# Weight loads of the expert stage in halves, with at most three halves on the way

## The chip, the core and the metric

The kernel runs on one core of a Trainium2 chip. The metric is the device time of one execution in microseconds (us). The core's engines work side by side, each through its own instruction stream: PE (TensorE, matrix products; PEld is its loading of weights), DVE (VectorE), ACT (ScalarE), POOL (GpSimd) and SP (SyncE). SP does nothing here but start transfers. All transfers between the chip's memory (HBM) and the core's memory (SBUF), whoever starts them, run on the same 16 DMA engines.

## The reference

Causal attention is followed by a mixture of experts with a capacity. Cut to what matters:

```python
# q, k, v: (8, 12, 448, 64); w1: (8, 768, 1024); w2: (8, 1024, 768); capacity 80
attn = softmax(causal(q @ k.T / 8)) @ v          # per batch and head
x = attn.transpose(0, 2, 1, 3).reshape(3584, 768)
logits = x @ w_gate                               # 8 experts
expert_idx = argmax(logits); gate_w = softmax(logits)[expert_idx]
for e in range(8):
    tok = the (at most) 80 tokens of expert e with the largest gate_w
    h = maximum(x[tok] @ w1[e], 0.0)
    out[tok] = gate_w[tok, None] * (h @ w2[e])    # all other rows stay zero
```

## The kernel before, in words

The first three quarters are the attention: scores, exponentials, transposes and products for 48 pairs of heads, in an order written out by hand, with the rows of x written to `xs` in HBM (L617), zeros to `out` (L305) and the gating worked out between. From about 355 us on come the eight experts, and only this stage is touched.

**Weights.** Each expert has a `w1` (768 x 1024) and a `w2` (1024 x 768) in f32. Both are cut into two *pieces* of 3072 columns on 128 partitions, 1.5 MB each (`PW`, `PIECES`: three chunks of 128 rows of `w1`, or four of `w2`): 32 pieces in all. `piece()` takes the next of ten buffers named `wraw` in turn. The first five pieces come in small parts during the attention (`piece_parts`, L213); five more come whole between 322 and 338 us; the other 22 are loaded by `split_pieces` while experts run. A load starts on SP's queue (`load_piece`, L202) when the piece that held its buffer ten pieces earlier has been used up.

**Splitting.** TensorE multiplies in f16 here, so each chunk of a piece becomes a high part `wh` (ScalarE, L1156) and a low part `wl` (VectorE, L1141, the scaled weight minus the high part). There are 12 buffers for high parts and 11 for low parts, so the two engines run ahead of PE by that many chunks. A few chunks (`whole`) are not split but multiplied in f32 straight from `wraw` (L1206).

**An expert.** GpSimd gathers the expert's 80 rows of x (`gather`, L1173) into `xg`. PE transposes them (`xtp`, L1187), ScalarE and VectorE split them into `xh` and `xl` (L1191, L1192). `layer1` makes the products with `w1`, three for each block of 128 x 128 (high by high, high by low, low by high: L1213, L1215, L1216). `hidden` applies the maximum and splits again (`hh` L1232, `hl` L1233). `layer2` does the same with `w2` into `op`. `outputs` scales (`yt`, L1279), transposes back (`ytp`, L1287), multiplies by the gate's weight (`yo`, L1291), and GpSimd scatters the 80 rows into `out` (L1294). Layer 1 of one expert runs before layer 2 of the expert before it.

**What sets the order.** PE's order in this stage is written out (`manual_schedule`). For the other engines a planner orders the instructions at build time, with its own costs, among those whose inputs and buffers it expects to be ready. Each engine then runs its list in order and waits on semaphores; a transfer raises its semaphore when all of it has landed. SP's list in this stage holds the 22 loads and the wait for the kernel's end.

Of the kernel before, what the change touches and what calls it, by code (L numbers as in the profile page):

```python
# [52 lines left out]
def attention_then_moe(  # L53
# [12 lines left out]
    nc = tc.nc  # L66
# [65 lines left out]
    for r in range(2):  # L132
        t = akeep.tile([P, OFF_L + NT * P], F32, name=f"prob{r}")
# [7 lines left out]
    for r in range(2):  # L141
        t = akeep.tile([P, NT, PH * P], F32, name=f"vt{r}")
# [20 lines left out]
        [(c, NT - 1, None) for c in (2, 1, 3, 0)],  # L163
    ]
    TB = 4

    PW = 3072
# [16 lines left out]
    def piece():  # L186

        e, which, c, k = PIECES[len(wload)]
        x = len(wload) % (WBUF + WMORE)
        pool, bufs = (wpool, WBUF) if x < WBUF else (wmore[0], WEARLY) if x < WBUF + WEARLY else (wmore[1], WMORE - WEARLY)  # L190
        t = pool.tile([P, k, PW // k], F32, name="wraw", tag="w", bufs=bufs)
        wload.append(t)
        return t, (w1 if which == 1 else w2)[e, :, c:c + k, :]

    def load_piece(behind=None):

        if len(wload) < len(PIECES):
            t, src = piece()
            if behind is not None:
                with tc.issue_after(behind.ins):  # L200
                    nc.gpsimd.memset(t[:, 0, 0:1], 0.0)
            nc.sync.dma_start(t, src)  # L202

    def piece_parts():

# [752 lines left out]
    with tc.manual_schedule():  # L958
# [26 lines left out]
        for i, pr in enumerate(pairs):  # L985
# [21 lines left out]
            for k in range(SLOTS):  # L1007
                behind = []
                if k < SLOTS - 1:
                    work, after = scores[k]  # L1010
                    turn, copy, x = turns[TSLOT.index(k)] if turns and k in TSLOT else (None, None, "a")
# [5 lines left out]
                    behind = [f for f in ((copy, after) if x == "a" else (after, copy)) if f]  # L1017
# [11 lines left out]
                if i == n - 2 and len(wload) >= WBUF and not parts and k in (0, 2, 4):  # L1029
                    load_piece()  # L1030
# [10 lines left out]
        while len(wload) < WBUF:  # L1041
            load_piece()
        while len(wload) < WBUF + WEARLY:
            load_piece()
# [40 lines left out]
        for i, x in enumerate(ROW_ENGINES):  # L1085
            g, t = divmod(i, NT)
# [30 lines left out]
    def whole(e, which, c):  # L1117

        if e >= E - 2:
            return False  # L1120
        return c == NC2 - 1 if which == 2 else c >= (NC1 // 2 if e == 0 else NC1 - 1)
# [11 lines left out]
    def split_pieces(m):  # L1133

        first = done[0]
        done[0] += m
        order, lows = [], []

        def low(l, src, h):
            with tc.issue_after((low_after or last_of)[-1].ins):  # L1140
                return nc.vector.scalar_tensor_tensor(out=l, in0=src, scalar=SW, in1=h, op0=ALU.mult, op1=ALU.subtract)  # L1141

        for i in range(first, first + m):
            while len(wload) <= i:
                load_piece()
            e, which, c, k = PIECES[i]
            for j in range(k):
                src = wload[i][:, j, :]
                order.append(c + j)
                if whole(e, which, c + j):  # L1150
                    parts_of[(e, which, c + j)] = (src,)
                    continue
                h = wsplit.tile([P, PW // k], F16, name="wh", tag="wh", bufs=HIS, padded_shape=[P, max(F, D)])
                l = wsplit.tile([P, PW // k], F16, name="wl", tag="wl", bufs=LOS, padded_shape=[P, max(F, D)])
                with tc.issue_after(batches[-1].raised.ins):
                    nc.scalar.activation(h, src, AF.Copy, scale=SW)  # L1156
                lows.append((l, lambda l=l, src=src, h=h: low(l, src, h)))
                parts_of[(e, which, c + j)] = (h, l)
        return order, lows

    def split_now(m):
        order, lows = split_pieces(m)
        for _, f in lows:
            f()
        return order
# [135 lines left out]
    for s in range(NSL):  # L1301
# [15 lines left out]
        with tc.manual_schedule(engines={mybir.EngineType.PE}):  # L1317
            for e in range(E + 1):
                if e < E:
                    u = units[e]  # L1320
                    if e == 0:

                        order, lows = split_pieces(n1)
                        u.order = order[NC1 // 2:] + order[:NC1 // 2]
                        units[1].order, more = split_pieces(n1)

                        with tc.issue_after(g.ins):
                            nc.gpsimd.memset(lows[0][0][:, 0:1], 0.0)
                        for nx in units[1:AHEAD]:
                            gather(nx)  # L1330
                        for _, f in lows:
                            low_after.append(f())
                        inputs(u)
                        low_after.append(u.xl)
                        for _, f in more:
                            f()
                    elif e > 1:
                        u.order = split_now(n1)
# [62 lines left out]
```

## Time and profile before

| | |
|---|---|
| time, median of 3 runs (lowest to highest) | 480.67 us (479.31 to 481.21) |
| the profiled execution: its time, its span | 479.74 us, 477.7 us |
| granted TensorE clock | 0.997 |
| busy, share of the span: PE, DVE, ACT, POOL | 93%, 86%, 83%, 67% |
| weight pieces loaded whole | 27, of 1536 KB, median 15.5 us from issue to landing |
| of these, while experts run | 22, issued from 360.2 to 432.7 us |
| moved in all | 120.88 MB, mean 253 GB/s |

The span runs from the first to the last instruction of the profiled execution; the device time is about 2 us longer. The shares are means over the attention and the experts, which have different limits, so a change in one stage is to be read from that stage's stretch of the span. A PE that counts as busy need not be at its peak, because its matrix products overlap and their ends are modelled.

### The profile page before, as it was taken

The page shows a single profiled execution, that of the slowest core. Times are in us where ns is not written, and L with a number is a line of the kernel's source. Part 1 is how long each engine was busy: PE and PEld are TensorE (multiplying, and loading weights), DVE is VectorE, ACT ScalarE, POOL GpSimd, SP SyncE. Part 2 cuts the span into 40 slices and gives each one's busy share as a digit, 9 for nine tenths or more (in the row PEclk, how much of TensorE's full clock was granted, in tenths as well). Part 3 has the DMA queues.
Part 4 walks back from the last instruction along what each step waited for, and adds up shares of the span by engine and source line. Part 5 has one row for each costly group of instructions (what it writes and reads, how often), then busy time and mean ns, then how long its engine had stood idle before and what let it go on. Part 6 is the DMA issues. An engine that isn't in the chain of part 4 may idle for free.

```text
span 477.7 us, 14801 instructions
## 1 busy us (share of the span) xinstructions
PE 444.4 (93%) x5290; PEld 341.8 (72%) x5290; DVE 412.1 (86%) x1264; ACT 398.4 (83%) x1075; POOL 319.9 (67%) x384
## 2 busy tenths in 40 slices
PE   3999989999999999999999999999989999998894
PEld 1676666767766776776677677777549998988894
DVE  6888798978987997897799789889479999999982
ACT  5998889879888887988888798888587999988982
POOL 7999999887987988798798879860254265401101
PEclk9999999999999999999999999999999999999998
DMA  7758998889669579866956886549938999999921
GB/s 219 178 148 230 278 313 235 248 248 297 184 195 293 159 224 264 245 187 196 291 159 218 257 253 181 186 134 337 424 125 272 392 390 387 390 424 428 418 73 43
DMA packets 43001, 120.88 MB, mean 253 GB/s; under 512 B 6146, under 2 KB 23810, under 8 KB 39472
## 3 DMA queue, kind: packets, MB, share of 16 engines
q1 hardware_dynamic: 41712, 116.21, 75.0%
q0 software_dynamic: 1056, 3.51, 2.4%
q8 instruction: 41, 0.67, 0.6%
q14 instruction: 32, 0.26, 0.2%
q10 hardware_dynamic: 160, 0.23, 0.2%
HBM read 96.36 MB, written 23.99 MB: 252 GB/s over the span
## 4 chain that ended last, share of the span: by engine, by line
PE 73%; DVE 10%; POOL 6%; issue 4%; ACT 4%; DMA 2%; POOLq 0%; SPq 0%; DVEq 0%; ACTq 0%
PE tp L466 14%; PE xp L496 13%; PE sp L424 6%; PE sp L425 5%; PE hp L1206 3%; ACT prob L449 3%; DVE ns L446 3%; PE rt L594 3%; PE hp L1215 3%; PE hp L1216 3%; PE hp L1213 3%; PE op L1213 3%; PE op L1215 3%; DMA qk<-k_t 2%; PE op L1216 2%
## 5 line engine op out<-in xcount | busy, mean ns | idle before, releaser
L449 ACT ACTIVATE prob<-ns,nb 128x128 f32<-128x128 f32 (+3 forms) x336 | 177.3, 530 | 35.6 <-DVE nb L446 34.0
L446 DVE CUSTOM_DVE_ANT_0 ns<-sp,mask 128x384 f32<-128x384 f32 (+2 forms) x288 | 116.0, 414 | 27.5 <-PE sp L425 15.8
L466 PE MATMUL tp<-ident,prob 128*128 128x128 f32 x768 | 119.9, 277 | 2.8 <-ACT prob L449 2.4
L478 ACT COPY PT<-tp 128x512 f32<-128x512 f32 x182 | 104.1, 572 | 12.3 <-PE sp L424 6.2
L396 POOL TENSOR_TENSOR qk<-qk,qk 128x448 f16<-128x448 f32 x92 | 97.4, 1078 | 13.3 <-DVE qk L388 7.1
L1141 DVE SCALAR_TENSOR_TENSOR wl<-wraw,wh 128x768 f16<-128x768 f32 (+1 forms) x98 | 97.9, 1059 | 5.2 <-ACT wh L1156 2.4
L466 PEld LDWEIGHTS tp<-ident,prob 128*128 128x128 f32 x768 | 89.6, 142 | 16.4 <-ACT prob L449 4.9
L496 PE MATMUL xp<-PT,vt 128*64 128x448 f32 (+3 forms) x768 | 91.1, 380 | 0.0
L1156 ACT ACTIVATE wh<-wraw 128x768 f16<-128x768 f32 (+1 forms) x98 | 84.7, 922 | 5.0 <-PE hp L1216 2.1
L496 PEld LDWEIGHTS xp<-PT,vt 128*64 128x64 f32 x768 | 53.8, 137 | 42.7 <-issue 22.6
L424 PE MATMUL sp<-qk 128*128 128x384 f16 (+2 forms) x288 | 75.7, 279 | 8.3 <-ACT qk L356 6.1
L425 PE MATMUL sp<-qk 128*128 128x384 f16 (+2 forms) x288 | 78.3, 278 | 1.6 <-DVE qk L350 1.6
L1215 PEld LDWEIGHTS <-wh 128*128 128x128 f16 x668 | 66.7, 100 | 4.4 <-issue 4.3
L1213 PEld LDWEIGHTS <-wh 128*128 128x128 f16 x668 | 67.1, 101 | 2.3 <-issue 2.3
L1294 POOL DMA_INDIRECT out<-yo,idx x8 | 21.4, 2676 | 68.2 <-ACT yo L1291 65.1
L1216 PEld LDWEIGHTS <-wl 128*128 128x128 f16 x668 | 66.7, 100 | 0.5 <-issue 0.5
L449 ACT ACTIVATION_READ_ACCUMULATOR prob<-ns,nb 128x1 f32 x336 | 64.3, 191 | 0.0
L391 POOL TENSOR_TENSOR qk<-qk,qk 64x448 f16<-64x448 f32 x46 | 51.3, 1115 | 4.1 <-POOL qk L350 0.6
L392 POOL TENSOR_TENSOR qk<-qk,qk 64x448 f16<-64x448 f32 x46 | 49.6, 1079 | 3.3
L385 POOL CAST qk<-qk 64x896 f16<-64x896 f32 x40 | 43.0, 1074 | 4.8 <-PE sp L437 3.6
L424 PEld LDWEIGHTS <-qk 128*128 128x128 f16 x288 | 28.5, 99 | 16.8 <-issue 7.3
L1213 PE MATMUL op<-hh,wh 128*128 128x80 f16 x324 | 37.1, 202 | 2.1 <-issue 2.1
(190 smaller groups left out, 899.8 us busy)
## 6 DMA issues: line engine op xcount, KB each, us to landing
wraw<-w SPq DMA_DIRECT2D x27, 1536.0 KB, 15.5
qk<-k_t SPq DMA_DIRECT2D x92, 224.0 KB, 5.5
out<-mask_l SPq DMA_DIRECT2D x56, 192.0 KB, 4.5
qk<-q_t SPq DMA_DIRECT2D x23, 448.0 KB, 4.3
vt<-v_t SPq DMA_DIRECT2D x24, 384.0 KB, 5.9
xs<-xr SPq DMA_DIRECT2D x42, 192.0 KB, 1.9
wraw<-w SPq DMA_DIRECT2D x24, 256.0 KB, 5.9
vt<-v_t SPq DMA_DIRECT2D x24, 64.0 KB, 5.6
```

The costliest lines, as they stand in the source:

```text
L396: nc.gpsimd.tensor_tensor(out=k_lo[j][:, i], in0=kf[j][:, i], in1=k_hi[j][:, i], op=ALU.subtract)
L424: nc.tensor.matmul(sp[:, 0:w], qx[:, p, t * P:w], kx[:, p, 0:w], start=True, stop=False)
L425: nc.tensor.matmul(sp[:, 0:w], qx[:, p, t * P:w], lx[:, p, 0:w], start=False, stop=True)
L446: pr.masked = nc.vector.tensor_tensor_reduce(out=ns[:, 0:w], in0=sp[:, 0:w], in1=m, scale=-1.0 / 8.0, scalar=HUGE, op0=ALU.add, op1=ALU.mi ...
L449: nc.scalar.activation(pr.P[:, off:off + w], ns[:, 0:w], AF.Exp, bias=nb, scale=-1.0, accum_out=total)
L466: nc.tensor.transpose(pr.tp[:, i], pr.P[:, off:off + P], ident)
L478: copy(dst, src)
L496: state["pe"] = nc.tensor.matmul(xp[rows, 0:w], st["vt"][:, c, p * P + j * DH:p * P + (j + 1) * DH], pr.PT[:, j, n0:n0 + w], start=(c == 0 ...
L1141: return nc.vector.scalar_tensor_tensor(out=l, in0=src, scalar=SW, in1=h, op0=ALU.mult, op1=ALU.subtract)
L1213: nc.tensor.matmul(o, wh[:, ws], ah[:, c, :], start=(x == 0 and i % per == 0), stop=False, skip_group_check=True)
L1215: nc.tensor.matmul(o, wh[:, ws], al[:, c, :], start=False, stop=False, skip_group_check=True)
L1216: nc.tensor.matmul(o, wl[:, ws], ah[:, c, :], start=False, stop=(x == n - 1), skip_group_check=True)
```

## The change

A piece that is loaded by `split_pieces` (22 of 32) goes in two transfers of 1536 columns, 0.75 MB each, instead of one; in HBM and in SBUF the 12 KB of a partition become two runs of 6 KB. Each of these halves waits on SP until the third half ahead of it in the list has landed, so that at most three halves are on the way at once. The first three don't wait. The wait for the buffer stays. Pieces loaded earlier are untouched.

```diff
+    HALVES = 3
...
-    def load_piece(behind=None):
+    on_way = []
+
+    def load_piece(behind=None, few=False):
 
         if len(wload) < len(PIECES):
             t, src = piece()
             if behind is not None:
                 with tc.issue_after(behind.ins):
                     nc.gpsimd.memset(t[:, 0, 0:1], 0.0)
-            nc.sync.dma_start(t, src)
+            if not few:
+                nc.sync.dma_start(t, src)
+                return
+            to, of = (x.rearrange("p k f -> p (k f)") for x in (t, src))
+            for x in (slice(0, PW // 2), slice(PW // 2, PW)):
+                got = nc.sync.dma_start(to[:, x], of[:, x])
+                if len(on_way) >= HALVES:
+                    tc.add_manual_dep(got.ins, on_way[-HALVES].ins.name, mybir.DependencyInfo(
+                        mybir.DependencyClass.Sync, mybir.DependencyReason.DATA), reason="halves on the way")
+                on_way.append(got)
...
             while len(wload) <= i:
-                load_piece()
+                load_piece(few=True)
```

## The prediction

> **What bounds the kernel now.** I read the page first (how busy the transfer engines are by slice), then the chain that ended last, then the stretches between its "issue" entries, then who waited for whom in the expert stage, then the weight loads.
>
> ```profile
> span 477.7 us, 14801 instructions
> DMA  7758998889669579866956886549938999999921
> ```
>
> The change touches only the expert stage, from 360 us on (slices 31 to 40). There the transfer engines are busy nine tenths and more until slice 38. In the chain, cut to 380:478 us (start, length, what), PE is the carrier, and entries named "issue" come back in it:
>
> ```profile
> 404.84 0.64 issue
> ...
> 411.38 0.39 issue
> ...
> 418.21 0.85 issue
> ...
> 436.55 1.47 issue
> ...
> 449.19 1.28 issue
> ...
> 456.42 0.25 issue
> ```
>
> "issue" means that PE waited for no semaphore that the profile shows. The ends of these entries (405.48, 411.77, 419.06, 438.02, 450.47) are a clue. Here are the stretches between such ends, with the instructions that PE and its weight loader ran in each:
>
> ```profile
> 398.74:405.48 6.74, 6.10 (x128) 5.96 (x129) 6.74 (x7) 6.26 (x10) 5.10 (x1) 1.00 1.01 361
> 405.48:411.77 6.29, 5.90 (x127) 5.80 (x128) 6.29 (x10) 5.43 (x10) 3.31 (x2) 1.00 1.01 420
> 411.77:419.06 7.29, 6.44 (x128) 6.33 (x128) 7.29 (x9) 6.54 (x10) 3.25 (x1) 1.00 1.02 376
> ...
> 438.02:444.21 6.19, 6.13 (x128) 6.02 (x128) 5.40 (x7) 5.04 (x7) 0.00 (x0) 1.00 1.03 431
> ...
> 457.00:461.00 4.00, 4.00 (x113) 3.99 (x112) 2.42 (x4) 3.68 (x8) 0.92 (x1) 1.00 0.23 66
> ```
>
> Columns: stretch, length, busy time and count of PE, PEld, DVE, ACT, POOL, granted clock, share of the transfer engines, GB/s. Each stall comes after 128 + 128 = 256 instructions, at full clock. The transfer queues show what else happens once per 256 instructions: of the stretch 425.31:438.02 (two periods), and of the tenth of a microsecond 435.5:435.6, the rows of queue 8 are
>
> ```profile
> q8 instruction: 2, 0.03, 1.1%
> ...
> q8 instruction: 1, 0.02, 67.6%
> ```
>
> One block of 0.02 MB of instructions starts at 435.5 and PE goes on at 438.02, some 2.5 us later. So while weights stream, PE is paced by the fetching of its own code: 6.2 to 7.3 us per 256 instructions. Once the weights are in (457:461) it runs 225 instructions in 4.00 us, 256 in 4.55, with no stall of that kind.
>
> Why is the fetch slow? The scatters, which share the transfer engines too, show it: first one beside the weight stream, then one without it (instruction, landing); then the transfers that ran between issue and first scatter packet, beside the stream (429.99:434.3) and without (469.2:470.6).
>
> ```profile
> L1294 POOL DMA_INDIRECT out<-yo,idx x1: 1226/1226/1226, 430.0 to 430.0; - x1
> ...
> DMA to landing us min/median/max: 8.5/8.5/8.5
> ...
> DMA to landing us min/median/max: 3.0/3.0/3.0
> ...
> DMA packets 168, 1.86 MB, mean 431 GB/s; under 512 B 17, under 2 KB 17, under 8 KB 17
> ...
> q1 hardware_dynamic: 168, 1.86, 102.3%
> ...
> DMA packets 0, 0.00 MB, mean 0 GB/s; under 512 B 0, under 2 KB 0, under 8 KB 0
> ```
>
> Beside the stream the scatter's descriptors are written by 431.2, and no scatter packet (q0) starts before 434.3: over 3 us. Without it, they are written by 470.1 (0.9 us) and the first comes after 470.6, in the next window: about 0.5. The stream adds some 2.6 us. One of its packets takes 16 x 4.31 x 1.023 / (168 - 17) = 0.47 us for 12 KB, so a newcomer waits behind 5 or 6 of them.
>
> Who loses by PE's pace? Waits in 360:468 us (waiter, what it waited for, total, times, longest) and the sum row of 360:468.2:
>
> ```profile
> DVE wl L1141 <- ACT wh L1156: 2.4, 3, 1.9
> ACT yo L1291 <- PE ytp L1287: 2.4, 3, 1.3
> ...
> ACT wh L1156 <- PE hp L1216: 2.1, 5, 0.8
> ...
> ACT yt L1279 <- PE op L1206: 2.0, 3, 1.1
> ...
> ACT wh L1156 <- PE op L1216: 1.9, 5, 0.7
> ...
> DVE wl L1141 <- ACT yt L1279: 0.6, 1, 0.6
> ...
> sum 108.20, PE 101.45 PEld 99.65 DVE 104.38 ACT 95.11 POOL 29.82; mean PE 101.45 PEld 99.65 DVE 104.38 ACT 95.11 POOL 29.82
> ```
>
> VectorE is the next bound, and close: 104.38 of 108.20 us busy, 3.82 idle. Of that, 3.0 (2.4 + 0.6) is behind ScalarE, whose own waits are for PE to free a buffer or deliver a product. No engine waits for a weight load.
>
> **The change part by part.** *22 loads become 44 halves.*
>
> ```profile
> L202 SPq DMA_DIRECT2D wraw<-w x22: 327/328/1005, 360.2 to 432.7; - x22
> ...
> DMA to landing us min/median/max: 8.0/17.0/25.1
> ...
> q1 hardware_dynamic: 3168, 34.60, 88.4%
> ```
>
> (The last row is of 360.15:457.72, when they run.) 22 more issues of 0.33 us are 7 us on SP, which issues nothing else here and has 97: nothing. *Packets shrink from 12 KB to 6 KB.* Their rate has two bounds: none lost; or the fixed part from the small packets of 200:300 us:
>
> ```profile
> q1 hardware_dynamic: 10938, 21.16, 72.1%
> ```
>
> Those are 16 x 100 x 0.721 / 10938 = 0.105 us each, completion marks included, for 1.9 KB. A line through both gives 0.035 us per KB and 0.04 fixed, so 8 more packets per engine and load cost 22 x 8 x 0.04 = 7 us at most. Packets there met others on the same engines, so I take the low side, 2 us more streaming.
>
> *Each half waits for the landing of the third ahead.* Queued behind that wait on SP are weight halves alone, and who waits for them are wh, wl and the unsplit products. At a landing two halves are still queued, 2 x 8 x 0.235 = 3.7 us of work. The turnaround to be hidden has two bounds:
>
> ```profile
> DMA to landing us min/median/max: 2.5/7.0/25.1
> ...
> DMA to landing us min/median/max: 23.6/23.6/23.6
> ...
> q1 hardware_dynamic: 2538, 27.85, 89.6%
> ```
>
> The first row is of all weight transfers; its shortest, 192 KB, took 2.5 us, of which 0.45 is moving: 2.0 fixed. The last counts 360.15:438.53, up to the landing of the 17th load (26.74 MB): 27.85 - 26.74 = 1.1 MB had been moved beyond it, 2.6 us at 420 GB/s, and with about 1 us from issue to first packet 3.6. Both are under 3.7, the upper just so. I take no bubble, because the average need is only 34.60 MB in 97.6 us, 355 GB/s, where three halves per (3.6 + 1.9) us give 430.
>
> *Cover for later landings.* The load issued at 410.6 landed 23.6 later (second row above), at 434.3, and its first rows were read at 436.8; the last, issued at 432.7, landed 25.0 later at 457.7 and was read from 463.1:
>
> ```profile
> 436.07 1.57 ACT L1156 ACTIVATE wh<-wraw 128x768 f16<-128x768 f32 x2
> ...
> 460.15 5.96 ACT L1156 ACTIVATE wh<-wraw 128x768 f16<-128x768 f32 x8
> ```
>
> (Second of the two and fifth of the eight.) So 2.5 us of cover at the tightest and 5.4 at the end, and a half more, 1.9 us, since the first rows need the first half alone. The 2 us are hidden; if 7 came instead, the rest would be paid.
>
> *What a newcomer waits behind.* If it waits behind a number of packets, 5 or 6 of 0.235 us cost 1.3 us instead of 2.6, and the fetch period drops from 6.2 to about 4.9. If it waits behind a number of bytes, nothing changes. I take the first: the two added delays are both near six packets, and in one row set bytes would do as well, so this is the step with the least behind it. How much is needed? PE ran 2219 + 2219 instructions in 360:468.2, 17.3 blocks; to keep out of VectorE's way (104.4 us) it needs 6.0 us per block on average, and now takes 6.2 to 7.3 while streaming. So 0.5 us would do in most blocks.
>
> Here a rule of the Trainium skill speaks against me. "Runtime: NRT & Kernel Launch", Instruction fetch mechanics, says that code is refilled in 16 KiB blocks of 256 instructions and that crossing a block is mostly hidden. The block size agrees with the 128 + 128 above; "hidden" does not, by the 0.25 to 1.47 us entries. If it held, the forecast would be the no-change rival.
>
> **Sum.** With PE out of the way VectorE gets back what it spends behind ScalarE: 3.0 of its 3.82 us. PE's whole "issue" time is not the gain, for VectorE then ends last; after its last wl nothing changes. The profiled execution took 479.74 us (span 477.7): 476.7. The median of the runs is 0.93 above it (480.67), so 477.7.
>
> **The rivals.** *No change (480.7).* The fetch waits behind bytes, or behind whole loads that are always present; PE stalls as before, and the loads stay hidden by the 2.5 us. For it: the engines stay as full as before. Against it: nothing in the trace, only the missing test with small packets. A part of the gain (478.5 to 480) counts here too.
>
> *Slower (486).* The window of three is too short: the turnaround is not 3.6 but 5.5 us, because each completion queues the way the scatter's first packet does (2.6 more, less what overlaps). Then three halves (2.36 MB) per 5.5 + 1.9 = 7.4 us give 319 GB/s, 34.60 MB take 108 us instead of 97.6, and of the 11 us the cover of 5.4 hides half: 480.7 + 5.5, about 486. It decides from a round of 6.6 us on, where 2.36 MB gives the 355 GB/s needed. For it: completion is already 2.6 us late. Against it: in the stretches where the stream is slowed by gathers, so are the two halves that cover.
>
> The Trainium skill, "DMA: Bandwidth & Descriptors", Bandwidth, asks for transfers of 1 MiB and more (its 1 MB row is 341 GB/s); by that alone 34.60 MB would take an estimated 101 us, inside the cover. No run here shows a half yet.
>
> *The change doesn't act.* If SP's own buffer waits already kept fewer than three halves on the way, the window would do nothing; but landings 17 us after issue at 4.4 us per load say four loads were queued. The halving acts in any case.
>
> **How the numbers follow.** Forecast 0.50 (with 475.5 to 478.3 as its own range: all 3.8 idle us gained and a median as low as the profiled run, or half of them); no change or a part 0.34; slower 0.16. Half a percent, 2.4 us, is about what runs of this kernel can tell from no change. The range runs from 475.5 to 485: it leaves out the worse half of the slow case and a sliver below.
>
> **What would show it.** Right: "issue" entries between 380 and 456 us shrink to few or none, stretches of 256 instructions take under 6 us, scatters beside the stream land in 6 to 7 us, ScalarE's waits for PE and VectorE's idle time (3.82) mostly vanish, the last wl ends about 3 us earlier. Wrong: stalls after every 256 instructions as before (no change); waits of wh or wl for a weight load, and a transfer share under 0.95 between 370 and 440 (slower).

## The result, and the profile after

The changed kernel takes 484.59 us (median of 4 runs, 484.23 to 485.77), the kernel before on the same chip 480.01 us (4 runs, 479.31 to 481.21). The ratio is 1.0082, with a 95% interval of 1.0057 to 1.0106: slower by 0.8%, where 477.7 us was forecast. The profiled execution took 484.23 us. In this kernel's lines, everything behind the diff stands 12 lines further down than before: `wh` is L1168, `wl` L1153, `xh` L1203, `xl` L1204; the halves are issued at L210.

From the page of the changed kernel:

```profile
span 482.2 us, 14857 instructions
...
DMA  7757997799769569777956967549839999999961
...
wraw<-w SPq DMA_DIRECT2D x44, 768.0 KB, 6.9
```

The transfer engines are now busy into slice 39, one slice longer. A half takes 6.9 us from issue to landing (median). The rows of line 210, and of the weight queue from the first issue to the last landing, 360.63:468.0:

```profile
L210 SPq DMA_DIRECT2D wraw<-w x44: 327/328/424, 360.6 to 461.2; - x44
...
DMA to landing us min/median/max: 5.3/6.9/9.6
...
q1 hardware_dynamic: 6336, 34.61, 87.9%
```

The same 34.6 MB need 107.4 us instead of 97.6, 322 GB/s instead of 355, and the last landing is 10.3 us later. What SP waited for, and who waited in the expert stage (345:482; the last two rows are PE's in 430:470):

```profile
SPq L210 <- DMA wraw<-w: 79.4, 40, 3.6
...
SPq L210 <- DVE wl L1153: 12.3, 5, 8.1
```

```profile
DVE wl L1153 <- ACT wh L1168: 5.4, 6, 1.4
ACT wh L1168 <- DMA wraw<-w: 4.8, 8, 1.5
...
PE hp L1225 <- ACT xh L1203: 4.0, 2, 3.1
PE hp L1227 <- DVE xl L1204: 1.5, 2, 1.0
```

All but the first three and one of the 44 halves waited at the window, and `wh` now waits for weight loads, which it did not do before. The stretches 380:430 and 430:460, first of before, then of the changed kernel, show when it went wrong:

```profile
380.00:430.00 50.00, 47.19 (x1005) 46.19 (x1001) 49.55 (x57) 45.11 (x70) 20.18 (x7) 1.00 1.01 399
430.00:460.00 30.00, 26.91 (x615) 26.30 (x614) 26.69 (x31) 26.05 (x39) 3.35 (x3) 1.00 0.87 362
```

```profile
380.00:430.00 50.00, 47.46 (x1009) 47.02 (x1008) 50.00 (x59) 44.78 (x71) 23.12 (x6) 1.00 0.99 363
430.00:460.00 30.00, 23.88 (x507) 23.24 (x506) 25.19 (x29) 24.68 (x36) 1.95 (x2) 0.91 0.98 361
```

Until 430 us the forecast's signs appear, but they are worth little: VectorE has no idle time at all (50.00 of 50.00), and before it idled only 0.45 us there, most of its 3.82 us coming after 430. Meanwhile only 363 GB/s arrive instead of 399, and the cover is eaten up. After 430 PE runs 507 products where it ran 615, and the granted clock is 0.91. In the chain the place looks like this (start, length, what), followed by ScalarE's list (ACT), in the view in order of time:

```profile
422.88 6.57 DMA wraw<-w
429.47 6.91 DMA wraw<-w
436.44 6.11 DMA wraw<-w
442.56 7.51 DMA wraw<-w
...
450.18 1.07 ACT wh L1168
...
455.21 0.66 DVE xl L1204
...
455.91 0.23 PE hp L1227
```

```profile
450.18 2.00 ACT L1168 ACTIVATE wh<-wraw 128x1024 f16<-128x1024 f32 x2 [1.47 <-DMA wraw<-w]
...
452.61 1.58 ACT L1168 ACTIVATE wh<-wraw 128x768 f16<-128x768 f32 x2
454.09 0.55 ACT L1203 ACTIVATE xh<-xtp 128x480 f16<-128x480 f32 x1
```

Four halves follow one another in the chain, each issued as the third ahead of it landed: the loads are the path from 422.9 to 450.1. ScalarE stands idle for 1.47 us at a late half; its waits of this kind add up to 4.5 us in 430:470. Behind it in its list, after four chunks of `wh` and one of `hh`, is `xh` of the next expert, small and independent of that load; PE can start nothing before `xh` and `xl`. So PE does almost nothing from 451.00 to 455.91, and then runs on half a clock (PE's busy time and count come first, the granted clock third from the end):

```profile
451.00:455.91 4.91, 0.84 (x7) 0.59 (x7) 4.64 (x7) 4.81 (x8) 0.00 (x0) 0.84 0.96 340
455.91:460.81 4.90, 4.90 (x72) 4.87 (x72) 4.90 (x6) 3.81 (x6) 0.00 (x0) 0.50 0.95 325
460.81:465.00 4.19, 4.19 (x104) 4.15 (x103) 2.92 (x5) 3.61 (x7) 0.91 (x1) 0.96 1.02 394
```

4.07 us of PE are lost in the first row and 2.45 (half of 4.90) in the second, 6.5 us together. The span grew by 4.5; against the loss stand the shorter stalls of PE, but the balance is not worked out further here.

The Trainium skill, "TensorE: Matmul & The Clock Gate", Part 1, says that the clock is halved after an idle window of about 3.4 us, until PE has been busy for about as long. The rows agree: 4.9 us with little work, then 4.9 us at 0.50, then 0.96. Worked out from the three rows, (1 - 0.84) x 4.91 / 0.5 + 4.90 + (1 - 0.96) x 4.19 / 0.5, the half clock lasted some 6.8 us, and in the first 1.6 of them PE still waited. A wait that idles PE for so long is paid for a second time.

### The profile page after: what moved, and what is told of

Its sections match the earlier page's. It is cut to its first block, busy times and chain, and to the rows that moved or that the text cites. A ratio compares the mean times of both kernels' runs of the same rounds, so it can differ in the third digit from the quotient of the medians.

```text
span 482.2 us, 14857 instructions
## 1 busy us (share of the span) xinstructions
PE 446.0 (92%) x5290; PEld 343.9 (71%) x5290; DVE 412.9 (86%) x1264; ACT 397.3 (82%) x1075; POOL 321.6 (67%) x384
## 4 chain that ended last, share of the span: by engine, by line
PE 61%; DVE 12%; DMA 12%; ACT 6%; issue 4%; POOL 3%; SPq 1%; POOLq 0%; DVEq 0%; ACTq 0%
PE tp L478 13%; PE xp L508 12%; DMA wraw<-w 8%; PE sp L436 5%; PE sp L437 4%; DMA qk<-k_t 4%; ACT prob L461 4%; DVE ns L458 3%; PE hp L1218 3%; PE rt L606 3%; PE hp L1227 2%; PE sp L446 2%; PE gp L558 2%; PE hp L1228 2%; PE hp L1225 2%
## 5 line engine op out<-in xcount | busy, mean ns | idle before, releaser
L1153 DVE SCALAR_TENSOR_TENSOR wl<-wraw,wh 128x768 f16<-128x768 f32 (+1 forms) x98 | 97.7, 1060 | 7.0 <-ACT wh L1168 5.4
L1168 ACT ACTIVATE wh<-wraw 128x768 f16<-128x768 f32 (+1 forms) x98 | 85.4, 925 | 7.6 <-DMA wraw<-w 4.8
L1227 PEld LDWEIGHTS <-wh 128*128 128x128 f16 x668 | 67.7, 101 | 5.1 <-issue 5.0
L1228 PEld LDWEIGHTS <-wl 128*128 128x128 f16 x668 | 67.7, 101 | 4.6 <-issue 4.6
L1306 POOL DMA_INDIRECT out<-yo,idx x8 | 23.0, 2881 | 70.2 <-ACT yo L1303 67.1
L1225 PEld LDWEIGHTS <-wh 128*128 128x128 f16 x668 | 68.2, 102 | 0.0
L1225 PE MATMUL hp<-xh,wh 128*128 128x80 f16 x320 | 38.3, 207 | 4.0 <-ACT xh L1203 4.0
L1227 PE MATMUL hp<-xl,wh 128*128 128x80 f16 x320 | 37.7, 207 | 4.0 <-DVE xl L1204 4.0
```

What stands on the lines that cost most here:

```text
L1225: nc.tensor.matmul(o, wh[:, ws], ah[:, c, :], start=(x == 0 and i % per == 0), stop=False, skip_group_check=True)
L1227: nc.tensor.matmul(o, wh[:, ws], al[:, c, :], start=False, stop=False, skip_group_check=True)
```

## The experiments

The changed kernel does three things: it halves the loads, limits them to three on the way, and, since the planner sees other transfers, reorders some rows of VectorE and ScalarE near the end (expert 6's `hh` and `hl` move behind expert 7's second `w1` piece). Theories: the window is too short (the slower rival); the order is to blame; small packets are. Beside them stands the open step of the prediction: does a newcomer wait behind packets or behind bytes? The kernel before took 480.5 us beside the first four, 481.06 beside the next four and 480.41 beside the last two.

**Halves without a window.**

```diff
-    HALVES = 3
+    HALVES = 99
```

> The halves alone: 44 loads of 0.75 MB, none waits for a landing (only for its buffer). Every engine's order is that of the changed kernel. If the window of three is what cost the 4.6 us (theory W: a round of three halves takes 6.1 to 7.5 us where 6.6 would just do), the loads move 34.6 MB in under 98 us again, no engine waits for a weight load, and the time is 477 to 481: 478 if smaller packets also shorten the fetch of PE's instructions, 480 if they don't. If the halves themselves are slow, by their packets (theory P) or by the order that the planner makes of them (theory O), it stays at 483 to 485.

479.65 us, ratio 0.9987 (0.9972 to 1.0001). The order is that of the changed kernel to the last instruction, so neither order nor halves cost 4 us: the window does. As for the newcomer: chain, line 210, and the transfers of 431.73:434.9, between a scatter's last descriptor and its first packet:

```profile
419.28 0.30 issue
...
425.50 0.33 issue
...
437.06 1.20 issue
...
449.44 1.01 issue
```

```profile
L210 SPq DMA_DIRECT2D wraw<-w x44: 327/328/1486, 360.9 to 443.8; - x44
...
DMA to landing us min/median/max: 7.7/15.5/19.0
...
q1 hardware_dynamic: 242, 1.33, 102.2%
```

PE stalls nearly as before (5.5 us in all, 6.3 before), and the scatter's first packet comes 3.2 us after its descriptors, against 3.1 to 3.25 before. Packets of 6 KB make no difference: 2.6 us of added delay are now 11 packets of 0.24 us instead of 5 or 6 of 0.47. So under a full queue the newcomer's wait is not set by a number of packets; whether by bytes or by time stays open.

**The window of three in the order of before.** The planner is told to put `hh` and `hl` of expert 6, and the pieces around them, where they were.

```diff
+    def split_around(p):
+        first = split_now(1)
+        hidden(p)
+        low_after.append(p.hl)
+        with tc.issue_after(p.hh.ins):
+            return first + split_now(1)
...
-                        u.order = split_now(n1)
+                        u.order = split_now(n1) if e < E - 1 else split_around(prev)
...
```

> The changed kernel with VectorE's list put back to that of the kernel before, and ScalarE's but for two splits that stay ahead of two output rows: expert 6's hidden parts again come ahead of expert 7's second weight piece. If the order cost the time (theory O), 480 to 481. If the window did (theory W), 483 to 485, and ScalarE still waits some 5 us for weight loads.

485.15 us, ratio 1.0106 (1.0075 to 1.0137), as slow as the changed kernel, with VectorE in the order of before and ScalarE in it but for two chunks:

```profile
ACT wh L1168 <- DMA wraw<-w: 9.8, 12, 1.7
```

The order is not the cause.

**No window, in the order of before.** `HALVES = 99` and a form of the same edit that brings back only part of the order (expert 7's `hl` stays two places late).

> Both taken away: halves without a window, in the order of the kernel before. Only 6 KB packets instead of 12 KB are left of the change. If the fetch of PE's instructions waits behind a number of packets (theory F), periods of 256 instructions fall below 6 us and the time to 476 to 478.5. If it waits behind bytes, it is 479.5 to 481, as before. Theory P says 483 to 485.

480.12 us, 0.9985 (0.9971 to 0.9998): the same as without the edit.

**A window of six halves.** `HALVES = 6`, 4.7 MB on the way.

> The changed kernel with a window of six halves (4.5 MB) instead of three. Theory W: a round of 6 halves has twice as long, 13.3 us at the rate needed, so nothing is lost and the time is within 1 us of the halves without a window. Theories P and O: 483 to 485.

478.99 us, 0.9969 (0.995 to 0.9988). `wh` waits 0.3 us for loads. PE's stalls are nearly as before (5.5 us).

**No loads at all.** The 22 loads are left out; pieces 10 to 31 are split from the buffers of pieces 6 to 9, so the products are of other weights.

```diff
-                load_piece(few=True)
+                wload.append(wload[(6 if PIECES[i][3] == K1 else 8) + i % 2])
```

> The 22 weight loads of the expert stage are left out; pieces 10 to 31 are split from the buffers of pieces 6 to 9, so the output is not the reference's. Work on every engine stays. It measures what freeing PE from the weight stream is worth at most. If PE's fetch under the stream is what VectorE loses its 3.8 idle us to (theory F), periods of 256 instructions come down to 4 to 5.5 us, VectorE's idle time in the stage to under 1.5, and the time to 476 to 477.5. If the fetch stalls cost nothing (rival: VectorE and ScalarE lose it to each other), 479.5 to 481.

476.48 us, 0.9907 (0.9884 to 0.9931): 4.6 us. The stretches 380:430 and 430:460:

```profile
380.00:430.00 50.00, 47.45 (x1020) 47.02 (x1016) 50.00 (x59) 45.78 (x72) 24.04 (x7) 1.00 0.10 28
430.00:460.00 30.00, 29.68 (x712) 29.46 (x711) 30.00 (x36) 29.71 (x46) 14.16 (x3) 1.00 0.07 20
```

VectorE is busy for 80.00 of 80 us (76.24 before). That is about all that the stream costs the expert stage, of which the forecast wanted 3.0: PE's stalls, and also what gathers and scatters lose beside it, which this run does not tell apart. A few places of VectorE's and ScalarE's order near the end differ as well.

**A window of four halves.** `HALVES = 4`.

> Four halves on the way instead of three; every list as in the changed kernel. Theory C (the cover decides: the bytes still queued when a landing lets the next load go): three halves are left, 2.36 MB or 5.6 us of work, against a turnaround of 4 to 5 us, so almost nothing is lost: 478.5 to 480.5, no wait of ScalarE for weights above 1 us. Theory B (a newcomer waits behind queued bytes, and only a queue shorter than what the engines take in ahead shortens that): about 1.6 MB stay unserved, a scatter's first packet comes 2.8 to 3.2 us after its descriptors. Rival N (the number of transfers on the way decides): 483.

479.47 us, 0.9973 (0.9955 to 0.999). One more half on the way, and the loss is gone. (Scatters beside the stream got their first packet after 2.0 to 3.1 us, where 2.8 to 3.2 was expected.)

```profile
ACT wh L1168 <- DMA wraw<-w: 0.3, 1, 0.3
```

**Whole pieces, two on the way.** In the order of before.

```diff
-    HALVES = 3
+    HALVES = 2
...
-            for x in (slice(0, PW // 2), slice(PW // 2, PW)):
+            for x in (slice(0, PW),):
```

> Whole pieces of 1.5 MB, as before the change and in its order, but each waits for the landing of the second ahead of it: two on the way, 3.1 MB, as many bytes as four halves. Theory C: when one lands, one piece is left, 1.57 MB or 3.7 us, the same cover as in the changed kernel, so the loads fall to 320 to 335 GB/s and the time is 482 to 486. If total bytes on the way decide, it is that of four halves, 478.5 to 480.5.

483.54 us, 1.0058 (1.0036 to 1.008). As many bytes on the way as with four halves (3.15 MB), but when one lands only one other, 1.57 MB, is queued, as in the changed kernel. The loss is back:

```profile
ACT wh L1168 <- DMA wraw<-w: 6.1, 6, 1.7
```

```profile
DMA to landing us min/median/max: 7.9/8.3/9.5
```

**Quarters, six on the way.** The same 2.36 MB as the changed kernel, but 1.97 MB queued at a landing.

```diff
-    HALVES = 3
+    HALVES = 6
...
-            for x in (slice(0, PW // 2), slice(PW // 2, PW)):
+            for x in (slice(i * PW // 4, (i + 1) * PW // 4) for i in range(4)):
```

> Quarters of a piece (0.375 MB, 3 KB packets) with six on the way: 2.36 MB in all, as in the changed kernel, in finer steps, so that 1.97 MB (4.6 us) are left at a landing instead of 1.57. The planner moves some 15 places of VectorE's and ScalarE's lists near the end. Theory C: the loads reach 335 to 350 GB/s, time 479 to 483. If total bytes decide, as the changed kernel: 483 to 486. Theory B: the scatter's first packet comes 1.5 to 2.8 us after its descriptors.

479.38 us, 0.9963 (0.9947 to 0.9978), with half the waits of the changed kernel:

```profile
ACT wh L1168 <- DMA wraw<-w: 2.6, 3, 2.0
```

**Quarters, five and seven on the way.** `HALVES = 5` and `HALVES = 7` with quarters; every engine's order is that of six.

> Each piece of the 22 goes in four quarters of 0.375 MB, and each quarter waits for the fifth ahead: 1.97 MB at most on the way, and 1.57 MB still queued when a landing lets the next one go. That is the cover of the changed kernel (two halves) and of the whole pieces with a window of two (one piece); the bytes at most on the way are less than in either (2.36 and 3.15 MB). Theory of cover (1.57 MB is 3.7 us of work, the turnaround is 4.5 to 5): as slow as those two, 483.5 to 485.5 us, with ScalarE waiting 4 to 10 us for weight loads. Rival, number of transfers on the way (two and three lose, four and more don't): five on the way are enough, 479 to 480 us as with six quarters. Rival, bytes at most on the way: the least of all kernels so far, so the slowest, 487 us and more.

> The same quarters, each waiting for the seventh ahead: 2.75 MB on the way, 2.36 MB queued at a landing. Every engine's order is that of the quarters with six and with five. Theory of cover: ScalarE's waits for weight loads (2.6 us with six quarters) are gone, and the queue is still shorter than the four or more whole loads of before, so PE's stalls for code are between those of six quarters and of halves with a window of four: 478.5 to 479.5 us. Rival, the queue's depth is all that counts for PE and the few waits of six quarters cost nothing: slower than six quarters, 479.5 to 480.5 us.

Five: 484.43 us, 1.0091 (1.0067 to 1.0116). Seven: 479.76 us, 0.9986 (0.9966 to 1.0005). With five, the two rows are

```profile
ACT wh L1168 <- DMA wraw<-w: 6.8, 10, 1.8
```

```profile
DMA to landing us min/median/max: 4.8/5.8/8.1
```

With seven `wh` does not wait for a load, but PE's stalls, 5.9 us, are not between those of six quarters (3.1) and four halves (4.6) as expected, and the time is the rival's, 479.5 to 480.5. The count of transfers is not what matters (five quarters lose, four halves don't), nor the bytes at most on the way (five quarters, 1.97 MB, are no worse than two pieces, 3.15 MB). What is still queued at a landing sorts all of them:

| kernel | on the way, MB | queued at a landing, MB | `wh` waits for loads, us | PE's waits of over 0.1 us for nothing visible, us | ratio to before |
|---|---|---|---|---|---|
| changed (3 halves) | 2.36 | 1.57 | 4.8 | 0.6 | 1.0082 |
| the same, order of before | 2.36 | 1.57 | 9.8 | 2.3 | 1.0106 |
| 2 pieces | 3.15 | 1.57 | 6.1 | 1.7 | 1.0058 |
| 5 quarters | 1.97 | 1.57 | 6.8 | 0.8 | 1.0091 |
| 6 quarters | 2.36 | 1.97 | 2.6 | 3.1 | 0.9963 |
| 4 halves | 3.15 | 2.36 | 0.3 | 4.6 | 0.9973 |
| 7 quarters | 2.75 | 2.36 | 0 | 5.9 | 0.9986 |
| 6 halves | 4.72 | 3.93 | 0.3 | 5.5 | 0.9969 |
| no window | by buffers | by buffers | 0.3 | 5.5 | 0.9987 |
| before | by buffers | by buffers | 0 | 6.3 | 1 |
| no loads | 0 | 0 | 0 | 0 | 0.9907 |

(The fifth column adds PE's idle times after 360 us that the trace puts down to "issue".) The stream, from the first issue to the end of its last packet, takes 106 to 109 us in the four kernels with 1.57 MB, 103 with 1.97, 98 to 101 with 2.36 and more, and 97 before. In 430:470 of the profiled executions the granted clock is 0.91 in the changed kernel, in the same in the order of before and with five quarters, 0.96 with two pieces and with six quarters, and 1.00 in all others. So the four slow kernels all lost clock; the one with six quarters lost some as well and was still not slower than before.

The two columns of waits run against each other: where the queue is short, PE's stalls shrink and the loads starve. That the code arrives sooner there is only in part shown, because PE then waits elsewhere, and such a wait can hide a stall: for `xh` and `xl` it waits 8.0 us in the changed kernel, 1.5 with six quarters, and not at all before. Between the two lies at best the 0.4% of six quarters, less than the half percent that the prediction calls tellable. Its interval overlaps those of its neighbours, but like those of four and six halves it lies below 1, so a small gain is likely.

## Why the prediction was wrong, point by point

**"The turnaround to be hidden has two bounds", 2.0 and 3.6 us, "both under 3.7": the step that failed first.** Issue to landing, less the moving of the transfer itself at 420 GB/s, is 6.9 - 1.9 = 5.0 us in the changed kernel, 5.8 - 0.9 = 4.9 with five quarters and 8.3 - 3.7 = 4.6 with two pieces (where the trace times only 5 of the 22 landings). So 4.6 to 5.0 us have to be hidden, above both bounds; 1.57 MB hide 3.7 us, 1.97 MB 4.7 and 2.36 MB 5.6, and that is where the loss fades and ends. The term that was too small is the "about 1 us" from issue to first packet. It is what the stage's first load took on an empty queue (0.96 us, before); under the stream it is another. Counting packets in order, 144 a half, shows it: up to the issue of the 30th half at 429.47, the queue had started

```profile
q1 hardware_dynamic: 4015, 21.97, 87.7%
```

of the 29 x 144 = 4176 packets ahead of it, and that half's first packet came at 431.68, 2.2 us later. Over all halves but the first four, 177 packets of the 288 of two halves had still to start at an issue (median), and the half's own first came 2.8 us after it. With two pieces and five quarters that is 2.8 and 2.7 us. So the landing's side was smaller than the 2.6 us taken (111 packets of 0.222 us on 16 engines, 1.5 us), issue to first packet was 2.8 instead of 1, and the two together come to 4.3 us, with 3.7 queued. (Engines can drift apart, so a count over all 16 is good to some tenths.) The row for a loaded queue stood next to the sum, the scatter's 3.1 us under the stream; it was used for the rival and not for the sum.

**The slower rival was the mechanism, and its size nearly right.** It had a round of 7.4 us, 319 GB/s, the deciding round at 6.6 us, and 486 us; measured are 6.9 us in the median, 322 GB/s and 484.59 us. It was given 0.16 because "in the stretches where the stream is slowed by gathers, so are the two halves that cover". But the bound stood 0.1 us from deciding against it, and a bound so close deserved an even chance.

**"If it waits behind a number of packets": the step that failed next.** The gain of 3.0 us rested on it, and 6 KB packets gained nothing of it without a window. The Trainium skill, "DMA: Bandwidth & Descriptors", Queues, rings and completion order, says that each engine goes round its queues packet by packet, by which halved packets should shorten a newcomer's wait; here the added 2.6 us stayed, so the wait is not one for the packet at work. What did shorten it is the short queue, though not every time: in the changed kernel five of the six scatters beside the stream got their first packet after 1.4 to 2.7 us (one after 3.1), in the order of before three of six after 2.1 to 2.4 (the others after 2.9 to 3.2). With six quarters, as many bytes on the way in packets of 3 KB, all took 1.3 to 2.2 us, so with a short queue a share of the packet size is not ruled out.

**"VectorE gets back what it spends behind ScalarE": not enough by itself.** With halves and no window PE's stalls stayed, and yet these two rows are all that the view of 360:468 lists of VectorE's waits, 1.0 us instead of 3.0 behind ScalarE:

```profile
DVE wl L1153 <- ACT wh L1168: 0.7, 3, 0.3
...
DVE wl L1153 <- ACT yt L1291: 0.3, 1, 0.3
```

Its last `wl` ended 1.6 us earlier (466.5 for 468.1), but the span stayed within 0.3 us (477.4 for 477.7): PE, still stalled, had 98 products to start after it instead of 74. So VectorE's waits need not follow PE's stalls, and here the time followed PE. These are single traces, but four halves and seven quarters show much the same (last `wl` at 466.0 in both, spans of 477.2 and 477.6).

**What held.** PE is stalled under the stream, 6.3 us in all, and not without it; with no loads VectorE fills its time and the kernel gains 4.6 us, so 3.0 was a fair size for the gain, had the stalls gone without a new wait. That the stalls are the code's fetch rests on their period of 256 instructions and on the queue of instructions; no run takes it apart from the rest of the stream's effect. The signs given appeared until 430 us: the stalls nearly gone, VectorE's idle time in 380:430 zero (0.45 before); a scatter issued at 430.3 landed in 7.1 us (8.5 before). The smaller packets cost 0.8 us of streaming (98.4 for 97.6, without a window), even less than the 2 taken. The 22 more issues cost nothing.

**"Who waits for them are wh, wl and the unsplit products": too short a list.** `xh` and `xl` stand in the same lists behind `wh` and `wl`, and through them PE waits, 5.5 us in 430:470, and loses its clock. In the sum this second price was missing.

**"A transfer share under 0.95": the wrong sign.** The share was 0.99 in 380:430 while the rate fell from 399 to 363 GB/s. Over all the loads, a packet (completion marks included) took 16 x 107.4 x 0.879 / 6336 = 0.238 us, and without a window, by this row of 360.9:459.3,

```profile
q1 hardware_dynamic: 6336, 34.61, 89.2%
```

16 x 98.4 x 0.892 / 6336 = 0.222. The lost time shows as longer packets of the same size, not as idle engines. They are few: from 361 to 462 us the median 6 KB packet took 0.23 us in both, but the longest 2.4 us in the changed kernel and 1.4 without a window. This fits waits that are recorded as part of a packet.

## What to carry to other kernels

A window on transfers is sized by what is still queued when one lands: those bytes at the stream's rate must outlast the turnaround measured under that same stream, from an issue behind a full queue to the semaphore (4.3 to 5.0 us here, so 2 MB and more), not that of a transfer on an empty queue. When a bound comes within a tenth of a microsecond of deciding, take both sides as equally likely. Read starving from GB/s and the waits, not from the busy share. And list what stands behind a waiting instruction in its engine's order, because an unrelated small step there can idle PE and cost it its clock as well.

## What the runs showed of the hardware that was not expected

A newcomer's delay under a full stream was the same with both packet sizes (12 KB: 3.1 to 3.25 us to the first packet, 6 KB: 3.2 to 3.3 with six halves or no window; 0.57 without a stream). Halves of 0.75 MB stream as well as pieces of 1.5 MB when enough are queued (98 us for 97); quarters of 0.375 MB took 101 us with seven on the way, at no cost to the kernel (479.76 us). And PE, idle for 4 of 4.9 us, was granted 0.50 of its clock for some 6.8 us, full clock again only after that.
